# Attention with two expert layers on one core: routing's intermediate values move into spare PSUM columns of the banks of the product with v

## The chip, the cores and the metric

The kernel runs on one core of a Trainium2 chip. The metric is the device time of one execution in microseconds (us). The core's engines run side by side, each through its own list of instructions in order: TensorE (PE, matrix products into PSUM), VectorE (DVE), ScalarE (ACT), GpSimd (POOL) and SyncE (SP, which issues most DMAs). They wait for each other by semaphores only.

## The reference, cut to what matters

```python
def reference(q, k, v, moe_w_gate, moe_w_output_gate, moe_w1, moe_w2, moe2_w_in, moe2_w_out):
    attn_out = causal_attention(q, k, v)          # 4 batches, 12 heads, 448 tokens, head size 64
    x = tokens by (head, size)                    # 1792 x 768
    logits = x @ w_gate                           # 8 experts
    e_idx = argmax(logits, axis=1)
    gate_w = softmax(logits)[e_idx]
    eom = 1 / (1 + exp(-(x @ w_output_gate)))
    for e in range(8):
        m = e_idx == e
        out[m] = gate_w[m] * eom[m, e] * (relu(x[m] @ w1[e]) @ w2[e])
    h = out @ w_in
    return (h - tanh(h)) @ w_out
```

## The kernel before, in words

The work has three stages. The first is attention (up to some 232 us of the profiled span), the second the eight experts over the tokens that were sent to each, the third the last layer, whose products are the end of the program.

Attention goes through 24 units (`u`, two heads of one batch each, six units to a batch). The unit loop is a pipeline written out by hand: in each round `u` there are six steps `m`, and in every step the engines are given a piece of several units: the scores of unit `u` (`s_mm`, L328 and L329), the transposes of the exponentials of unit `u - 1` (`t_mm`, L361), the product with v of unit `u - 2` (`v_mm`, L380), and the transposes and logits of units `u - 3` and `u - 4` (`g_mm` L429, `g_lg` L440 and L441). DVE takes row maxima (L335), copies odd transposes (L367) and divides (L391, L394, L398); ACT takes the exponentials (L343), copies even transposes (L369, L431) and scales the second head (L402); POOL splits values into high and low halves (L302, L408, L409) and prepares weights (L117, L131). The order of the instructions on each engine is the order of this code; nothing reorders it.

The product with v of a unit has two result tiles, one for each head `h`, `[112, 4, 65]` in float32, 260 of the 512 columns of a PSUM bank. Steps 0 to 2 write head 0 (`VM` and `VO` set this), steps 3 to 5 head 1. Both come from the pool `ps_o` with two buffers, so head 0 always gets one bank and head 1 the other.

After a batch's last logits are added up (L447, L449), `routing(b)` runs for that batch as a generator: each `yield` ends a piece, and the loop takes one piece at every even step, in rounds `u` = 9 to 13 for the first batch, 15 to 19 for the second and 21 onwards for the third; the fourth (`b` = 3) runs after the last unit without other attention work beside it. The pieces are: add high and low logits, take the maximum (L453, L455); exponentials and comparison (L459 to L463); the one-hot choice (L466, L468); the running rank by matmuls and three DVE operations (L490 to L499); rank to place (L503 to L506); the weight of the token (L473 to L482, with an exponential on ACT at L476); the index table (L512 to L536). The intermediate values `lg`, `eq`, `es`, `rk`, `pi` and `pf` are tiles of the SBUF pool `sm`, three buffers each, as are `mx`, `ex`, `m2`, `eo`, `sx` and `bi`.

Of the kernel before, what the change touches and what calls it, by code (L numbers as in the profile page):

```python
# [12 lines left out]
F32 = mybir.dt.float32  # L13
F16 = mybir.dt.float16
BF16 = mybir.dt.bfloat16
I32 = mybir.dt.int32
# [4 lines left out]
PSUM = bass.MemoryType.PSUM  # L21
SP = mybir.EngineType.SP

B, H, S, D = 4, 12, 448, 64
CP, NCH = 112, 4
NT, DM = B * S, H * D
E, F1 = 8, 1024
# [32 lines left out]
def build(ctx: ExitStack, tc: tile.TileContext, kq0, kq, v, wg, wo, w1, w2, wf, out):  # L60
# [120 lines left out]
    with ExitStack() as actx:  # L181
# [3 lines left out]
        sm = sctx.enter_context(tc.tile_pool(reuse_waits="tile", name="sm", bufs=3, side="right"))  # L185
# [50 lines left out]
        NS = HU * S  # L236
        ps_s = actx.enter_context(tc.tile_pool(reuse_waits="tile", name="ps_s", bufs=3, space=PSUM))
        ps_t = actx.enter_context(tc.tile_pool(reuse_waits="tile", name="ps_t", bufs=3, space=PSUM))
        ps_o = actx.enter_context(tc.tile_pool(reuse_waits="tile", name="ps_o", bufs=2, space=PSUM))

        def views(z):
            stage = (raw1.rearrange("p a b -> p (a b)")[:, 2048:] if z % 2 else raw2.rearrange("p a b -> p (a b)"))
# [128 lines left out]
        def v_mm(u, h, i):  # L371
            d = st_[u]
            hl = (u % 2) * 2 + h
            if ("o", h) not in d:
                d["o", h] = ps_o.tile([128, 512], F32, tag="o", name=f"o_{u}_{h}")[:CP, 0 : NCH * (D + 1)].rearrange(
                    "p (c d) -> p c d", c=NCH)
            po = d["o", h]
            for j in range(i + 1):
                g, o = where[(h, i, j)]
                nc.tensor.matmul(out=po[:, i, :], lhsT=d["PT"][:, g, o : o + CP], rhs=d["t"][3][:, hl, j, :], start=(j == 0),  # L380
                                 stop=(j == i))
# [67 lines left out]
                nc.vector.tensor_tensor(out=lga, in0=lga, in1=plg, op=ALU.add)  # L449

        def routing(b):
            lg = sm.tile([CP, NCH, 2 * E], F32, tag="lg", name=f"lg_{b}")
            nc.vector.tensor_tensor(out=lg, in0=lga[:, :, 2 * E :], in1=lga[:, :, 0 : 2 * E], op=ALU.add)  # L453
            mx = sm.tile([CP, NCH, 1], F32, tag="mx", name=f"mx_{b}")
            nc.vector.tensor_reduce(out=mx, in_=lg[:, :, 0:E], op=ALU.max, axis=AX.X)  # L455
# [2 lines left out]
            ex = sm.tile([CP, NCH, E], F32, tag="ex", name=f"ex_{b}")  # L458
            nc.vector.tensor_tensor(out=ex, in0=lg[:, :, 0:E], in1=mxb, op=ALU.subtract)  # L459
            nc.scalar.activation(out=ex, in_=ex, func=AF.Exp, scale=1.0 / LSC)  # L460
            eq = sm.tile([CP, NCH, E], F32, tag="eq", name=f"eq_{b}")
            nc.vector.tensor_tensor(out=eq, in0=lg[:, :, 0:E], in1=mxb, op=ALU.is_equal)
            nc.vector.tensor_tensor(out=eq, in0=eq, in1=desc.unsqueeze(1).to_broadcast([CP, NCH, E]), op=ALU.mult)  # L463
            yield
# [6 lines left out]
            def weight():  # L471
                eo = sm.tile([CP, NCH, E], F32, tag="eo", name=f"eo_{b}")
                nc.vector.tensor_tensor(out=eo, in0=lg[:, :, E:], in1=ohb, op=ALU.mult)  # L473
                es = sm.tile([CP, NCH, 1], F32, tag="es", name=f"es_{b}")
                nc.vector.tensor_reduce(out=es, in_=eo, op=ALU.add, axis=AX.X)
                nc.scalar.activation(out=es, in_=es, func=AF.Exp, scale=-1.0 / LSC)  # L476
                sx = sm.tile([CP, NCH, 1], F32, tag="sx", name=f"sx_{b}")
                nc.vector.tensor_reduce(out=sx, in_=ex, op=ALU.add, axis=AX.X)
                yield
                nc.vector.tensor_scalar(out=es, in0=es, scalar1=1.0, scalar2=YSC, op0=ALU.add, op1=ALU.mult)  # L480
                nc.vector.scalar_tensor_tensor(out=es, in0=sx, scalar=1e-9, in1=es, op0=ALU.add, op1=ALU.mult)
                nc.vector.reciprocal(out=tm[:, b * NCH : (b + 1) * NCH, 1:2], in_=es)  # L482
                yield
# [7 lines left out]
            for c in range(NCH):  # L491
                nc.tensor.matmul(out=prv[:, c + 1 :, :], lhsT=onesb[:CP, :CP],
                                 rhs=oh[:, b, c : c + 1, :].to_broadcast([CP, NCH - c, E]), start=False, stop=(c == NCH - 1))
            rk = sm.tile([CP, NCH, E], F32, tag="rk", name=f"rkm_{b}")
            nc.vector.tensor_tensor(out=rk, in0=prv[:, 0:NCH, :], in1=base.unsqueeze(1).to_broadcast([CP, NCH, E]), op=ALU.add)
            nc.vector.tensor_tensor(out=rk, in0=rk, in1=oh[:, b, 0:NCH, :], op=ALU.mult)
            rb = rank[:, b * NCH : (b + 1) * NCH]
            nc.vector.tensor_reduce(out=rb.unsqueeze(2), in_=rk, op=ALU.add, axis=AX.X)
            nc.vector.tensor_tensor(out=base, in0=base, in1=prv[:, NCH, :], op=ALU.add)  # L499
            yield  # L500
            pi = sm.tile([CP, 3, NCH], I32, tag="pi", name=f"pi_{b}")
            pf = sm.tile([CP, 2, NCH], F32, tag="pf", name=f"pf_{b}")
            nc.vector.tensor_copy(out=pi[:, 0, :], in_=rb)  # L503
            nc.vector.tensor_scalar(out=pi[:, 2, :], in0=pi[:, 0, :], scalar1=7, scalar2=None, op0=ALU.logical_shift_right)
            nc.vector.tensor_scalar(out=pi[:, 1, :], in0=pi[:, 0, :], scalar1=127, scalar2=None, op0=ALU.bitwise_and)
# [2 lines left out]
            if b < B - 1:  # L508
                yield from weight()
# [4 lines left out]
            e = nc.vector if b >= B - 2 else nc.gpsimd  # L514
# [92 lines left out]
        for u in range(NU + 5):  # L607
# [20 lines left out]
            for m in range(6):  # L628
# [21 lines left out]
                if ok(u - 2):  # L650
                    for z in VM[m]:
                        v_mm(u - 2, *VO[z])
# [47 lines left out]
                if ok(u - 4) and (u - 4) % 6 == 5 and m == 2:  # L700
                    route = routing((u - 4) // 6)
# [561 lines left out]
    for q in range(2):  # L1263
        to_f32([(qc[q][:, h], stg[q][:, h, :]) for h in HS])
        for z in range(2):
            for h in HS:
                c = qc[q][:, h].bitcast(F32)
# [110 lines left out]
    for n in range(NF + 3):  # L1378
        g, f = divmod(n, KF2)
# [87 lines left out]
```

## Time and profile before

| | us |
|---|---|
| median of 3 runs | 1032.12 |
| lowest and highest | 1030.98, 1037.31 |
| the profiled execution, its own time | 1036.02 |
| its span, first to last instruction | 1034.3 |

| engine | busy us | share of the span | instructions |
|---|---|---|---|
| PE (matmul) | 981.5 | 95% | 8985 |
| PEld (weight loads of PE) | 735.5 | 71% | 8985 |
| DVE | 785.0 | 76% | 1704 |
| ACT | 604.1 | 58% | 1213 |
| POOL | 467.3 | 45% | 504 |

A row of the timeline gives the start, the time that the instruction or group took, the engine, the line, the operation, the result and its inputs, and in brackets how long the engine had sat idle before it and what ended that. Matmuls overlap each other, so their times add to more than they take together. An idle time is put down to the last of the things waited for.

### The profile page before, as it was taken

Reading aid. Unit: us, or ns where it says so; the run is one execution under the profiler, and the core shown is the slowest. Engines: PE = TensorE matmul, PEld = TensorE weight load, DVE = VectorE, ACT = ScalarE, POOL = GpSimd, SP = SyncE. Lnnn points to the kernel's source line nnn. Section 1 sums busy time; section 2 is a strip of 40 time slices with the busy share of each in tenths; the row PEclk is TensorE's granted clock in tenths of the full one; section 3 lists DMA queues with packets and bytes.
Section 4 is the critical chain, followed back from the end, with each engine's and each line's share of the span. In section 5 each row is a group of like instructions: output and inputs, shape, how many; then the busy total and the mean of one; then the engine's idle time right before and its main releaser. Section 6 shows DMA issues by size and latency. Waiting matters only on the chain. (4 is left out here: it accounts for less than half of the span.)

```text
span 1034.3 us, 23797 instructions
## 1 busy us (share of the span) xinstructions
PE 981.5 (95%) x8985; PEld 735.5 (71%) x8985; DVE 785.0 (76%) x1704; ACT 604.1 (58%) x1213; POOL 467.3 (45%) x504
## 2 busy tenths in 40 slices
PE   5989999999899998998998899999999999999996
PEld 3989999988678786686876455666666666667763
DVE  6647878787887778668886999887888798776640
ACT  5658887765456365564334698565556566555530
POOL 5466776575211021122136689645544443443321
PEclk9979999999999999999999999999999999999999
DMA  8888999954998988988986360010000000000000
GB/s 244 232 200 232 268 263 224 258 188 144 327 338 333 359 277 303 339 295 300 323 321 220 130 273 1 31 40 16 23 32 31 8 32 8 16 16 16 16 24 23
DMA packets 62648, 173.94 MB, mean 168 GB/s; under 512 B 8368, under 2 KB 23344, under 8 KB 59424
## 3 DMA queue, kind: packets, MB, share of 16 engines
q1 hardware_dynamic: 56352, 147.20, 42.5%
q0 software_dynamic: 6144, 24.84, 8.7%
q8 instruction: 80, 1.31, 0.5%
q14 instruction: 72, 0.59, 0.2%
HBM read 132.30 MB, written 29.62 MB: 157 GB/s over the span
## 5 line engine op out<-in xcount | busy, mean ns | idle before, releaser
L1361 PE MATMUL fo<-wo,g 128*128 128x384 f16 x1344 | 228.2, 326 | 0.0
L1310 PEld LDWEIGHTS <-raw 128*128 128x128 f16 x1440 | 141.2, 98 | 86.7 <-issue 9.0
L1361 PEld LDWEIGHTS <-g 128*128 128x128 f16 x1344 | 131.2, 98 | 83.8
L1320 POOL TENSOR_TENSOR V<-cu,cc 128x384 f32<-128x384 f32 (+1 forms) x80 | 80.1, 1001 | 188.0 <-ACT cu L1319 185.4
L164 PEld LDWEIGHTS <-w 128*128 128x128 f16 x2592 | 146.0, 98 | 9.5 <-issue 8.1
L1310 PE MATMUL fh<-cu,raw 128*128 128x384 f16 (+1 forms) x864 | 133.1, 310 | 4.6 <-DVE cc L1318 3.4
L380 PE MATMUL o<-v,PT 112*112 112x65 f32 x960 | 119.4, 266 | 0.0
L343 ACT ACTIVATE P<-s,nb 112x112 f32<-112x112 f32 (+1 forms) x192 | 89.8, 495 | 49.5 <-DVE nb L335 24.9
L380 PEld LDWEIGHTS o<-v,PT 112*112 112x112 f32 x960 | 110.3, 185 | 0.2
L123 DVE SCALAR_TENSOR_TENSOR w<-raw,w 128x768 f16<-128x768 f32 (+1 forms) x99 | 99.0, 1060 | 11.4 <-ACT w L115 11.4
L335 DVE CUSTOM_DVE_ANT_0 s<-s,maskw 112x112 f32<-112x112 f32 (+1 forms) x192 | 85.8, 459 | 21.4 <-PE s L329 18.4
L811 POOL DMA_INDIRECT xg<-xs_d,idx x22 | 30.7, 1397 | 155.9 <-PEq L886 36.5
L1319 ACT ACTIVATE cu<-cc 128x384 f32<-128x384 f32 (+1 forms) x80 | 40.0, 500 | 93.9 <-DVE cc L1318 93.9
L115 ACT ACTIVATE w<-raw 128x768 f16<-128x768 f32 (+2 forms) x106 | 89.4, 904 | 6.7 <-DMA raw<-w 3.9
L1318 DVE TENSOR_TENSOR cc<-fh,co 128x384 f32<-128x384 f32 (+1 forms) x80 | 42.0, 525 | 63.5 <-PE fh L1310 50.8
L1323 POOL TENSOR_TENSOR X<-cc,X 128x384 f32<-128x384 f32 (+1 forms) x80 | 87.6, 1094 | 4.1 <-ACT X L1322 0.5
L1330 DVE SCALAR_TENSOR_TENSOR V<-cu,V 128x384 f32<-128x384 f32 (+1 forms) x80 | 82.6, 1032 | 0.1
L1338 DVE TENSOR_TENSOR V<-V,co 128x384 f32<-128x384 f32 (+1 forms) x64 | 77.5, 1211 | 0.0
L361 PE MATMUL t<-ident,P 112*112 112x112 f32 x480 | 69.3, 268 | 0.0
L1310 PE MATMUL fh<-yh,raw 128*128 128x384 f16 x384 | 67.6, 326 | 0.7 <-DVE cc L1318 0.7
L1339 ACT ACTIVATE g<-V 128x384 f16<-128x384 f32 (+1 forms) x80 | 40.0, 500 | 45.9 <-DVE V L1338 45.7
L328 PE MATMUL s<-kh,qa 128*112 128x112 f16 (+1 forms) x192 | 54.4, 302 | 12.8 <-POOL qa L280 7.3
(670 smaller groups left out, 1978.3 us busy)
## 6 DMA issues: line engine op xcount, KB each, us to landing
raw<-w SPq DMA_DIRECT2D x48, 512.0 KB
raw<-w SPq DMA_DIRECT2D x60, 384.0 KB
cu<-wf SPq DMA_DIRECT2D x22, 1024.0 KB
wb_d<-co SPq DMA_DIRECT2D x22, 512.0 KB
raw<-kq SPq DMA_DIRECT2D x11, 896.0 KB
raw<-wb_d SPq DMA_DIRECT2D x8, 768.0 KB
xs_d<-xq SPq DMA_DIRECT2D x24, 224.0 KB
raw<-v SPq DMA_DIRECT2D x11, 448.0 KB
```

What stands on the lines that cost most here:

```text
L115: nc.scalar.activation(out=out, in_=in_, func=AF.Copy, scale=WS)
L123: nc.vector.scalar_tensor_tensor(out=out, in0=in_, scalar=WS, in1=hi, op0=ALU.mult, op1=ALU.subtract)
L164: nc.tensor.matmul(out=ph[:, (f % 4) * 128 : (f % 4 + 1) * 128], lhsT=w[0][:, ww, k, f * 128 : (f + 1) * 128], rhs=xTs[tag][:, xx, k, :], ...
L335: nc.vector.tensor_tensor_reduce(out=d["s", m][:, z, :], in0=d["s", m][:, z, :], in1=maskw[:, S - n : S], scale=-0.125, scalar=3.0e38, op0 ...
L343: nc.scalar.activation(out=d["P"][:, j, OFF[i] : OFF[i] + n], in_=d["s", m][:, z, :], func=AF.Exp, bias=d["nb"][:, 2 * i + j : 2 * i + j + ...
L380: nc.tensor.matmul(out=po[:, i, :], lhsT=d["PT"][:, g, o : o + CP], rhs=d["t"][3][:, hl, j, :], start=(j == 0), stop=(j == i))
L1310: nc.tensor.matmul(out=ph[:, 0:nt], lhsT=wi[ww][:, f // 4, k, f % 4 * 128 : (f % 4 + 1) * 128], rhs=yy[:, k, 0:nt], start=(q == 0), stop=( ...
L1320: nc.gpsimd.tensor_tensor(out=d["V"], in0=d["U"], in1=d["h"], op=ALU.mult)
L1323: nc.gpsimd.tensor_tensor(out=d["X"], in0=d["h"], in1=d["X"], op=ALU.subtract)
L1330: nc.vector.scalar_tensor_tensor(out=d["V"], in0=d[f"S{z}"], scalar=QD[z - 1], in1=d["V"], op0=ALU.add, op1=ALU.mult)
L1338: nc.vector.tensor_tensor(out=d["V"], in0=d["V"], in1=rs_y(g, nt), op=ALU.mult)
L1361: nc.tensor.matmul(out=po[:, 0:384], lhsT=t[:, x, k, i * 128 : (i + 1) * 128], rhs=wo_[ww][:, k, z * 384 : (z + 1) * 384], start=(k == 0 a ...
```

## The change

Routing's `lg`, `eq`, `es`, `rk`, `pi` and `pf` are no longer SBUF tiles. They lie in columns 320 to 475 of the PSUM bank that holds head 0 of the product with v. The two result tiles of that product, until now a new pair from a rotating pool for every unit, become two tiles that are made once, `o_0` and `o_1`. Each value has one place now where it had three buffers.

```diff
-        ps_o = actx.enter_context(tc.tile_pool(reuse_waits="tile", name="ps_o", bufs=2, space=PSUM))
+        ps_o = actx.enter_context(tc.tile_pool(reuse_waits="tile", name="ps_o", bufs=1, space=PSUM))
+        o_ps = [ps_o.tile([128, 512], F32, name=f"o_{h}") for h in range(2)]
+        small = lambda o, n: o_ps[0][:CP, 320 + o : 320 + o + n]
...
-                d["o", h] = ps_o.tile([128, 512], F32, tag="o", name=f"o_{u}_{h}")[:CP, 0 : NCH * (D + 1)].rearrange(
-                    "p (c d) -> p c d", c=NCH)
+                d["o", h] = o_ps[h][:CP, 0 : NCH * (D + 1)].rearrange("p (c d) -> p c d", c=NCH)
...
-            lg = sm.tile([CP, NCH, 2 * E], F32, tag="lg", name=f"lg_{b}")
+            lg = small(0, NCH * 2 * E).rearrange("p (c e) -> p c e", c=NCH)
...
-            eq = sm.tile([CP, NCH, E], F32, tag="eq", name=f"eq_{b}")
+            eq = small(64, NCH * E).rearrange("p (c e) -> p c e", c=NCH)
...
-                es = sm.tile([CP, NCH, 1], F32, tag="es", name=f"es_{b}")
+                es = small(128, NCH).unsqueeze(2)
...
-            rk = sm.tile([CP, NCH, E], F32, tag="rk", name=f"rkm_{b}")
+            rk = small(96, NCH * E).rearrange("p (c e) -> p c e", c=NCH)
...
-            pi = sm.tile([CP, 3, NCH], I32, tag="pi", name=f"pi_{b}")
-            pf = sm.tile([CP, 2, NCH], F32, tag="pf", name=f"pf_{b}")
+            pi = small(132, 3 * NCH).bitcast(I32).rearrange("p (a n) -> p a n", a=3)
+            pf = small(144, 2 * NCH).rearrange("p (a n) -> p a n", a=2)
```

No engine's instructions change their order. What changes is which of them wait, since routing's values now share a bank with the products with v. In the rows below the names with a number are tiles; `o_172` is `o_0`, the fixed tile of head 0. The lines of the changed kernel are one or two higher than those of the kernel before.

On PE, in round 11 of the unit loop, the end of step 1, first before and then after; `lg_1691` and `lg_1668` are the logits of a later unit, `v_4` and `PT` the inputs of the product with v of unit 9:

```order
L440 LDWEIGHTS xh_1634
L440 MATMUL lg_1691<-wgc,xh_1634 128x32
L441 LDWEIGHTS xh_1634
L441 MATMUL lg_1691<-wgc,xh_1634 112x16
L380 MATMUL o_0_1662<-v_4_957,PT_1475 112x65 x3
L328 LDWEIGHTS qa_1001
L328 MATMUL s_2_1709<-kh_1002,qa_1001 112x336 [waits Activation_49]
```

```order
L441 LDWEIGHTS xh_1613
L441 MATMUL lg_1668<-wgc,xh_1613 128x32
L442 LDWEIGHTS xh_1613
L442 MATMUL lg_1668<-wgc,xh_1613 112x16
L381 MATMUL o_172<-v_4_950,PT_1459 112x65 [waits Activation_49]
L381 MATMUL o_172<-v_4_950,PT_1459 112x65 x2
L330 LDWEIGHTS qa_993
L330 MATMUL s_2_1686<-kh_994,qa_993 112x336
```

The product with v, which waited for nothing here, waits for ACT (for the exponential of `es`, L476), and the next scores, which waited for ACT, need no wait of their own any more.

On DVE, in the same round, the end of step 0 with the first operations of the token's weight, first before and then after; `rs_1` belongs to the division of head 1, `o_173` is `o_1`, `eo`, `oh`, `sx` and `ex` are still SBUF tiles:

```order
L391 TENSOR_SCALAR rs_1_1668<-o_1_1583 112x4
L394 RECIPROCAL rs_1_1668<-rs_1_1668 112x4 [waits DVE_49]
L473 TENSOR_TENSOR eo_1671<-lg_1403,oh 112x32
L475 TENSOR_REDUCE es_1673<-eo_1671 112x4 [waits DVE_49]
L478 TENSOR_REDUCE sx_1676<-ex_1446 112x4
```

```order
L392 TENSOR_SCALAR rs_1_1646<-o_173 112x4
L395 RECIPROCAL rs_1_1646<-rs_1_1646 112x4 [waits DVE_49]
L474 TENSOR_TENSOR eo_1649<-o_172,oh 112x32 [waits PE_49]
L476 TENSOR_REDUCE o_172<-eo_1649 112x4 [waits DVE_49]
L479 TENSOR_REDUCE sx_1653<-ex_1431 112x4
```

`eo`, which waited for nothing, waits for PE (for the product with v of step 0), because its input `lg` now lies in the bank that this product writes.

## Rows read from the trace of the kernel before

**Rows 1.** The page, part 1: busy us of each engine (share of the span) xinstructions.

```profile
PE 981.5 (95%) x8985; PEld 735.5 (71%) x8985; DVE 785.0 (76%) x1704; ACT 604.1 (58%) x1213; POOL 467.3 (45%) x504
```

**Rows 2.** Windows: length, then busy us (instructions) of PE, PEld, DVE, ACT, POOL; clock, DMA.

```profile
133.00:180.00 47.00, 45.71 (x504) 43.11 (x503) 38.51 (x153) 35.99 (x90) 32.70 (x38) 1.00 0.95 251
```

**Rows 3.** Waits between 90 and 260 us: waiter <- waited for: us, times, longest.

```profile
PEld t L361 <- ACT PT L369: 0.6, 2, 0.3
...
PE s L328 <- ACT P L343: 0.6, 2, 0.3
...
PE rk L490 <- DVE oh L468: 0.5, 1, 0.5
...
PE xt L429 <- DVE base L499: 0.2, 1, 0.2
```

**Rows 4.** DVE groups by shape, 90 to 260 us: busy us, mean ns | idle before.

```profile
L496 DVE TENSOR_TENSOR rkm<-rkm,oh 112x32 f32<-112x32 f32 x4 | 5.0, 1253 | 0.1
...
L453 DVE TENSOR_TENSOR lg<-lga 112x64 f32<-112x64 f32 x4 | 3.6, 894 | 0.1
...
L462 DVE TENSOR_TENSOR eq<-lg,mx 112x32 f32<-112x32 f32 x4 | 2.2, 546 | 0.0
...
L463 DVE TENSOR_TENSOR eq<-eq,desc 112x32 f32<-112x32 f32 x4 | 1.7, 422 | 0.1
L473 DVE TENSOR_TENSOR eo<-lg,oh 112x32 f32<-112x32 f32 x4 | 1.7, 415 | 0.0
...
L504 DVE TENSOR_SCALAR pi<-pi 112x4 int32<-112x4 int32 x4 | 1.3, 334 | 0.1
...
L506 DVE CAST pf<-pi 112x8 f32<-112x8 int32 x4 | 1.2, 303 | 0.1
...
L495 DVE TENSOR_TENSOR rkm<-rk,base 112x32 f32<-112x32 f32 x4 | 0.8, 192 | 1.4 <-PE rk L492 1.3
...
L475 DVE TENSOR_REDUCE es<-eo 112x4 f32<-112x32 f32 x4 | 0.7, 186 | 0.1
```

**Rows 5.** Timeline, second batch's rank: DVE, then POOL, then PE.

```profile
157.46 2.51 DVE L496 TENSOR_TENSOR rkm<-rkm,oh 112x32 f32<-112x32 f32 x1
...
158.04 1.88 POOL L302 TENSOR_TENSOR lo<-raw,t 128x896 f16<-128x896 f32 x1
...
160.41 0.55 PE L429 MATMUL xt<-identh,xq 112*128 112x112 f16 x8 [0.25 <-DVE base L499]
```

**Rows 6.** Timeline, second batch's weight: PE, then ACT.

```profile
164.12 0.78 PE L380 MATMUL o<-v,PT 112*112 112x65 f32 x6
165.21 0.30 PE L328 MATMUL s<-kh,qa 128*112 128x336 f16 x1 [0.31 <-ACT P L343]
...
165.66 0.20 ACT L476 ACTIVATE es<-es 112x4 f32<-112x4 f32 x1
```

**Rows 7.** Timeline, first batch: choice (DVE, PE), then weight (DVE, ACT, PE).

```profile
102.98 0.19 DVE L468 TENSOR_TENSOR oh<-eq,m 112x32 bf16<-112x32 f32 x1
...
103.21 0.78 PE L380 MATMUL o<-v,PT 112*112 112x65 f32 x6
...
111.00 0.82 DVE L473 TENSOR_TENSOR eo<-lg,oh 112x32 f32<-112x32 f32 x1
...
112.08 0.21 ACT L476 ACTIVATE es<-es 112x4 f32<-112x4 f32 x1 [0.89 <-DVE es L475]
...
111.78 0.78 PE L380 MATMUL o<-v,PT 112*112 112x65 f32 x6
```

**Rows 8.** Timeline of PE: first scores of rounds 17, 18, 21 and 22.

```profile
161.90 0.21 PE L328 MATMUL s<-kh,qa 128*112 128x112 f16 x1
...
170.94 0.21 PE L328 MATMUL s<-kh,qa 128*112 128x112 f16 x1
...
196.03 0.21 PE L328 MATMUL s<-kh,qa 128*112 128x112 f16 x1
...
204.32 0.21 PE L328 MATMUL s<-kh,qa 128*112 128x112 f16 x1
```

## The prediction

> **What bounds the kernel now.** I read the page's busy times first. PE is busy for 95% of the span, the next engine, DVE, for 76% [rows 1]. The change touches attention alone, so I then read the windows of that stage: between 133 and 180 us, a stretch that holds nearly all of the routing of the second batch, PE is busy for 45.71 of 47 us at full granted clock, DVE for 38.51 [rows 2]. The reader is to see that PE sets the pace there and that DVE, which does nearly all of routing, has some 8 us to spare in 47. What DVE saves is therefore worth only what PE waits for because of DVE, and the list of waits is the third view. Between 90 and 260 us PE lost little to DVE or ACT: twice 0.3 us for exponentials of L343, twice 0.3 us for a copy of L369, 0.2 us for the running base of L499, and 0.5 us for the one-hot choice of the last batch [rows 3].
>
> The fourth view, the groups by shape, tells why DVE is late at all. L496 multiplies 32 columns and takes 1253 ns on average, L495, the same operation on the same shape just before it, 192 ns [rows 4]. They differ in one thing: L495 has one input in PSUM and one in SBUF, L496 both in SBUF. The timeline shows the disturbance: the L496 of the second batch runs from 157.46 for 2.51 us and ends 0.05 us after POOL's L302, which works on SBUF from 158.04 for 1.88 us [rows 5]. L462, L463, L473, L504 and L506 are long in the same way [rows 4].
>
> **What the change removes.** In L462, L463, L473 and L496 one of two SBUF inputs becomes a PSUM input, in L504 and L506 everything lies in PSUM. If they then behave like L495, the four cost 192 ns each. Over four batches that is (1253 - 192) x 4 = 4.2 us for L496, (546 - 192) x 4 = 1.4 for L462, 0.9 for L463 and 0.9 for L473. For L504 and L506, against the 186 ns of the small reduction L475, it is (334 - 186) x 4 = 0.6 and 0.5. The sum is 8.5 us of DVE time [rows 4]. L453 keeps both inputs in SBUF and stays at 894 ns.
>
> Of these 8.5 us PE gets only what it waited for. Round 17 of the unit loop, in which the second batch's weight is computed, takes 170.94 - 161.90 = 9.04 us, round 21, without such a wait, 204.32 - 196.03 = 8.29 us [rows 8]. The 0.75 us between them hold one each of the 0.3 us waits for L343 and L369, whose other halves fall in the third batch [rows 3]. So I count 0.75 us twice, and 0.2 us for L499, which came late because of the long L496 [rows 3, 5]: 1.7 us gained, at most.
>
> What would a write to PSUM cost? No row shows a small DVE operation with input and output in PSUM. The nearest rows are L495 (PSUM to SBUF, 192 ns) and L475 (SBUF to SBUF, 186 ns) [rows 4]: no difference that matters, and I take none. From below, nothing can make them much shorter than that; from above I allow 50 ns on each of some 20 operations, 1 us of DVE time per batch, which the 8 us that DVE has to spare in rows 2 hide in the first three batches. In the last one six of them stand ahead of the choice that PE waits for [rows 3], 0.3 us.
>
> [...]
>
> **What the change adds.** No instruction moves; waits are added, since the values share a bank with head 0 of the product with v. Three kinds matter.
>
> First, DVE waits for PE: L453, L466, L473 and L480 wait for the last product into that bank. Behind them stand DVE's copies and row maxima, for which ACT waits. In the first batch L473 began at 111.00 after the product with v of step 0, so this costs nothing when DVE is on time.
>
> Second, PE waits for DVE: the products of head 0 at steps 0 and 1 wait for L463, L468, L506 and L517 where they waited for the division L398 or for nothing. Behind them stands all of PE. The closest is the choice: L468 ended at 102.98 + 0.19 = 103.17 and the product began at 103.21 [rows 7]. The margin is 0.04 us. I take 0.1 us a batch for it, 0.3 us in all; from below it is 0, with the time saved at L462 and L463 ahead of it.
>
> Third, PE waits for ACT: the product of step 1 in the weight's round waits for the exponential L476, which waits for L475 and L473. In the first batch L476 began at 112.08 and the product at 111.78, so as things stand this is a new wait of 112.29 - 111.78 = 0.5 us. But L473 took 0.82 us there, and ACT had sat idle for 0.89 us until L475 came [rows 7]. With L473 at 0.19 us the chain is 111.00 + 0.19 + 0.19 + 0.21 = 111.59, before the product. I take 0.1 us a batch, 0.3 us in all.
>
> The waits of DVE for itself, and the 1.4 KB per partition that become free (three buffers of 480 bytes) and shift other tiles, I cost at nothing: nothing else is placed or loaded differently, and DVE's spare time covers the first. The fourth batch has no product with v beside it and takes none of the three waits.
>
> **The sum.** -1.7 + 0.3 + 0.3 = -1.1 us on the profiled execution's 1036.02 us, that is 1034.9. The profiled execution lies 3.9 us above the median of the runs shown, 1032.12; the same step from the median gives 1031.0. The runs themselves spread over 6.3 us (1030.98 to 1037.31), so about 1%, 10 us, is what a measurement of this kernel can tell from no change, and this is far less.
>
> **Rivals.**
>
> The new waits win (slower). Place: the product with v of step 1 in the weight's round, behind L476. Point: it decides as soon as L475 ends more than 0.19 us later than in the chain above (111.78 - 111.59), because DVE stays late, be it by L453, which keeps its length, or because an operation with one SBUF operand is still held up by POOL. This second reason means that the change does not do what it says. Price, with DVE as late as before: in the second batch the product can start only at 165.66 + 0.20 = 165.86 instead of 164.12, and the scores behind it after its 0.78 us at 166.64 instead of 165.21, 1.4 us [rows 6]; the third batch as much, the first 0.5 us: 3.3 us. The products of step 0 and the choice can add as much again, 6.6 us. Midway, +5 us: 1041 by the profile, 1037 on the median's scale. For it speaks that in rows 6 ACT is late on its own account too; against it, that rows 7 show the chain in time but for one disturbed operation.
>
> [...] That the program guards the whole bank is seen in the order of PE, where the product got a wait for columns it does not touch; no trace here shows what would happen without.
>
> All of PE's idle time goes (faster). DVE early by 8.5 us might also shorten waits that are put down to POOL or ACT. The cap is PE's idle time in the window, 47 - 45.71 = 1.3 us for a batch [rows 2], 3.9 us for three; taking 3 us gives 1029. Against it: part of that idle time is issue and the wait for POOL's halves, which the change leaves alone.
>
> The time saved in attention is lost again behind it, since the experts' weights come at their own pace: 0 us, 1032.1. Nothing in rows 2 speaks against it; it cannot be told from the forecast.
>
> **How the numbers follow.** Chances: forecast 0.5 (its own range 1029 to 1034), saved and lost again 0.2, new waits win 0.18, all idle time goes 0.12. All of them lie within 1% of 1032.12 by their price. For a median of few runs I add 2 us on either side of 1029 and 1 us above 1037: 1027 to 1038. More than 10 us faster would need more than the 8.5 us of DVE time that is to be had, chance 0.03, left for what I have not seen; more than 10 us slower would need the dearest form of the waits and half as much again, 0.04; within 1%: 0.93.
>
> **What would show it right or wrong.** In the changed kernel's profile L496 (one line lower) should take about 192 ns in all four batches, like L462, L463 and L473, while L453 stays long; busy DVE should fall by some 8 us and busy PE stay. Round 17 should take about 8.4 us. PE's list of waits should have new rows of a few tenths for L380 on ACT L476 and DVE L468. If DVE's operations are still over a microsecond, the first part is wrong; if L380 waits over 1 us a batch, the second; if the time differs by over 10 us, something outside attention changed, and the whole reading is wrong.

## The result and the profile after

| | kernel before | changed kernel |
|---|---|---|
| median of 6 runs each, us | 1034.79 | 1021.13 |
| lowest and highest, us | 1030.98, 1037.31 | 1016.89, 1022.43 |
| ratio to before, 95% interval | | 0.9866, 0.9838 to 0.9894 |
| the profiled execution, its own time and its span, us | 1036.02, 1034.3 | 1016.89, 1015.2 |

The changed kernel is faster by 1.3%. The forecast was 1031.0 us, the range 1027 to 1038: both are wrong. The operations did what was forecast of them. What their lateness had cost was read much too low.

The page of the changed kernel, part 1, answers to [rows 1]:

```profile
PE 971.3 (96%) x8985; PEld 728.7 (72%) x8985; DVE 776.7 (77%) x1704; ACT 604.1 (60%) x1213; POOL 462.4 (46%) x504
```

DVE is busy for 8.3 us less, the forecast's 8. PE, which was to stay, is busy for 10.2 us less with the same 8985 matmuls. The same matmuls in less busy time point to the clock, and this is the first sign of what the prediction left out: over the whole span the mean granted clock is 0.982 before and 0.991 after. Most of that difference lies in one place of this profile of before, round 6, to which the first experiment comes.

DVE's groups by shape between 90 and 260 us, as in [rows 4] (lines are one or two higher, a result named `o` lies in the fixed tile):

```profile
L454 DVE TENSOR_TENSOR o<-lga 112x64 f32<-112x64 f32 x3 | 2.5, 847 | 0.4 <-PE o L381 0.4
L496 DVE TENSOR_TENSOR o<-rk,base 112x32 f32<-112x32 f32 x4 | 0.8, 200 | 1.7 <-PE rk L493 1.7
L464 DVE TENSOR_TENSOR o<-o,desc 112x32 f32<-112x32 f32 x4 | 0.8, 199 | 0.1
L497 DVE TENSOR_TENSOR o<-o,oh 112x32 f32<-112x32 f32 x4 | 0.8, 199 | 0.1
L463 DVE TENSOR_TENSOR o<-o,mx 112x32 f32<-112x32 f32 x4 | 0.8, 197 | 0.0
L507 DVE CAST o<-o 112x8 f32<-112x8 int32 x4 | 0.7, 174 | 0.1
L505 DVE TENSOR_SCALAR o<-o 112x4 int32<-112x4 int32 x4 | 0.7, 170 | 0.1
L474 DVE TENSOR_TENSOR eo<-o,oh 112x32 f32<-112x32 f32 x4 | 0.7, 163 | 0.0
```

Each of these but L454 takes 163 to 200 ns, where they took up to 1253. L454, the old L453, has both inputs in SBUF still and is still long.

The timeline of the second batch's rank, DVE and POOL, answers to [rows 5]: L497 takes 0.20 us beside the same operation of POOL that held it for 2.51 us before.

```profile
147.91 0.20 DVE L497 TENSOR_TENSOR o<-o,oh 112x32 f32<-112x32 f32 x1
...
148.01 1.89 POOL L304 TENSOR_TENSOR lo<-raw,t 128x896 f16<-128x896 f32 x1
```

PE's list of waits between 90 and 260 us, as in [rows 3] (waiter, waited for, us, times, longest):

```profile
PE pt_I-4341_4342 L151 <- DMA xg<-xs_d,idx: 1.5, 1, 1.5
PE py_I-4366_4367 L176 <- issue: 0.6, 1, 0.6
PE rk L491 <- DVE oh L469: 0.5, 1, 0.5
PE s L331 <- DMA kl<-lo: 0.3, 1, 0.3
PE px L531 <- DVE bb L522: 0.2, 1, 0.2
```

The waits for ACT's exponentials, for its copies and for the running base are gone; the one of the last batch's choice stays at 0.5 us. The product with v (L381) is not in the list, whose shortest row is 0.2 us: none of the waits that the change added holds PE for longer than that. A wait that [rows 3] do not show is gone too. In the same list of before it was the longest one of PE for DVE:

```profile
PE px L530 <- DVE bb L521: 0.8, 1, 0.8
```

It stands before the product that starts the third batch's index table. The 0.2 us of L531 that the list after shows belong to the fourth batch.

The window of 47 us with the second batch, as in [rows 2] (PE busy, then PEld, DVE, ACT, POOL, clock, DMA):

```profile
125.00:172.00 47.00, 46.62 (x526) 44.77 (x524) 36.20 (x156) 37.13 (x94) 32.25 (x36) 1.00 0.96 249
```

PE's idle time falls from 1.29 to 0.38 us. That is 0.9 us for a batch, the size that the prediction had in mind. So between these two profiles the routing of the second batch explains very little of the 13 us, and the experiments had to find the rest.

### The profile page after: what moved, and what is told of

Its sections match the earlier page's. It is cut to its first block, busy times and chain, and to the rows that moved or that the text cites. A ratio compares the mean times of both kernels' runs of the same rounds, so it can differ in the third digit from the quotient of the medians.

```text
span 1015.2 us, 23805 instructions
## 1 busy us (share of the span) xinstructions
PE 971.3 (96%) x8985; PEld 728.7 (72%) x8985; DVE 776.7 (77%) x1704; ACT 604.1 (60%) x1213; POOL 462.4 (46%) x504
## 5 line engine op out<-in xcount | busy, mean ns | idle before, releaser
L381 PE MATMUL o<-v,PT 112*112 112x65 f32 x960 | 115.3, 260 | 0.0
L381 PEld LDWEIGHTS o<-v,PT 112*112 112x112 f32 x960 | 106.1, 179 | 0.3
L812 POOL DMA_INDIRECT xg<-xs_d,idx x22 | 27.0, 1228 | 153.1 <-PEq L887 29.5
```

## The experiments

All of them are read by one yardstick as well: the time from the first scores of round 10 to those of round 19, in which the routing of the first two batches runs. The length of a round is the difference between the starts of its first scores and of the next round's, as in [rows 8].

| kernel | routing's values in | rounds 10 to 18, us | clock there | round 11 | round 17 | DVE busy, page |
|---|---|---|---|---|---|---|
| before | SBUF | 78.37 | 1.00 | 8.82 | 9.04 | 785.0 |
| again | SBUF | 85.45 | 0.94 | 11.51 | 13.19 | 788.3 |
| again2 | SBUF | 86.39 | 0.94 | 14.95 | 11.36 | 792.0 |
| fixed_only | SBUF | 80.91 | 1.00 | 9.80 | 9.92 | 788.2 |
| shift_only | SBUF | 80.18 | 0.98 | 8.29 | 11.57 | 785.2 |
| fill | SBUF | 80.77 | 1.00 | 10.05 | 9.99 | 789.5 |
| rk_only | one of six in PSUM | 78.83 | 1.00 | 8.64 | 9.84 | 786.1 |
| all_but_rk | five of six in PSUM | 78.19 | 1.00 | 8.68 | 8.51 | 777.5 |
| late | PSUM | 79.86 | 1.00 | 9.58 | 9.86 | 781.8 |
| changed | PSUM | 76.81 | 1.00 | 8.42 | 8.52 | 776.7 |
| changed_again | PSUM | 76.71 | 1.00 | 8.42 | 8.51 | 777.0 |
| changed_pad | PSUM | 75.93 | 1.00 | 8.44 | 8.51 | 776.7 |
| lg_copy | PSUM | 79.17 | 1.00 | 8.29 | 8.94 | 777.1 |
| lg_copy2 | PSUM | 78.49 | 1.00 | 8.29 | 8.51 | 776.4 |

### The kernel before, profiled again (again, again2)

The span of before held one dear event that has nothing to do with routing. In round 6, in which no routing runs, PE waited for a DMA, and its clock then fell (timeline of PE, and in the second fence two windows of before with the clock in the third column from the right):

```profile
61.73 0.25 PE L329 MATMUL s<-kl,qa 128*112 128x112 f16 x1 [2.59 <-DMA kl<-lo]
```

```profile
60.00:70.00 10.00, 8.27 (x51) 8.09 (x52) 3.03 (x14) 3.62 (x11) 3.74 (x6) 0.56 0.93 239
70.00:80.00 10.00, 10.00 (x88) 9.36 (x87) 5.52 (x22) 5.17 (x13) 5.92 (x7) 0.76 0.86 219
```

Round 6 took 17.2 us instead of 8.3. The first question was whether the change removes this, whether its fixed tiles or addresses matter, or whether it is an accident of that execution. The first repetition asked this, together with the three kernels of the next section:

> The kernel before, unchanged, to see whether the wait of 2.6 us for the transfer of kl at round 6 and the half clock behind it (1.2 GHz until about 75 us, round 6 17.2 us instead of 8.3) belong to it. Theory A (the gain of the changed kernel is this one wait and its clock, taken away by a steady part of the change): round 6 takes about 17 us here too, time ratio 1.00. Theory B (the wait is an accident of one profiled execution): round 6 takes 8.3 us here, and the ratio is still 1.00, so that the 13 us of the changed kernel must come from elsewhere.

Measured: 1031.58 us (10 runs, 1025.16 to 1038.49), ratio 1.0019 (0.9975 to 1.0063). Round 6 took 8.30 us here, and in every other profile between 8.30 and 8.53. The event was an accident of one execution, and not what the change removes.

But two other rounds were dear, 11 and 17, both with the weight of a token. The second repetition had a theory of this on record, theory D: operations of routing with their inputs in SBUF make DVE late, and PE waits behind it. Theory B has the first measurement of the changed kernel as an accident.

> The kernel before, unaltered, another profile. Theory D: PE waits for ACT or DVE by 0.3 to 1.5 us in at least one of rounds 11, 14, 16 and 17, and rounds 10 to 18 take 78 to 86 us together. Theory B: rounds 10 to 18 take 75.5 to 77.5 us, like the changed kernel.

Measured: 1032.17 us (12 runs), ratio 1.0003 (0.9965 to 1.004), rounds 10 to 18 in 86.39 us, 0.4 us above the range that the theory of late operations expected. Its timeline shows the mechanism at its clearest, in round 11: DVE, then POOL, then ACT, then PE.

```profile
100.25 0.17 DVE L504 TENSOR_SCALAR pi<-pi 112x4 int32<-112x4 int32 x1
100.33 1.88 DVE L505 TENSOR_SCALAR pi<-pi 112x4 int32<-112x4 int32 x1
102.24 3.07 DVE L506 CAST pf<-pi 112x8 f32<-112x8 int32 x1
105.22 0.62 DVE L335 CUSTOM_DVE_ANT_0 s<-s,maskw 112x448 f32<-112x448 f32 x1
...
100.29 1.89 POOL L302 TENSOR_TENSOR lo<-raw,t 128x896 f16<-128x896 f32 x1 [2.59 <-DMA xs_d<-xq]
...
103.33 1.89 POOL L302 TENSOR_TENSOR lo<-raw,t 128x896 f16<-128x896 f32 x1
...
105.93 0.63 ACT L343 ACTIVATE P<-s,nb 112x448 f32<-112x448 f32 x1 [4.59 <-DVE nb L335]
...
106.61 0.30 PE L328 MATMUL s<-kh,qa 128*112 128x336 f16 x1 [3.01 <-ACT P L343]
```

L505 and L506 work on 4 and 8 columns. L505 ends at 102.21, 0.03 us after the first L302 of POOL, L506 at 105.31, 0.09 us after the second. The row maxima (L335) behind them come late, ACT sits idle for 4.59 us and PE for 3.01. The two are no exceptions: in the six profiles with all of routing's values in SBUF, 120 of routing's operations on at most 64 columns take more than 0.35 us between 80 and 262 us, and every one of them ends between 0.02 us before and 0.16 us after the end of an instruction of POOL. No run took POOL's work away, so that POOL is what holds them rests on these ends, and on the operations that became short when their values moved. Then the clock falls (windows of again2):

```profile
106.00:108.00 2.00, 1.39 (x12) 1.08 (x11) 1.90 (x12) 1.94 (x7) 0.00 (x0) 0.98 1.13 283
108.00:114.00 6.00, 6.00 (x30) 5.28 (x30) 4.66 (x19) 4.79 (x12) 5.01 (x6) 0.50 1.01 347
114.00:116.00 2.00, 2.00 (x23) 1.87 (x22) 0.69 (x2) 0.98 (x2) 1.89 (x3) 0.81 1.07 338
```

For 6 us and a part of the next two PE is never idle, and yet its granted clock is 0.50, the lower of the two values that the clock takes in the traces of before and of the changed kernel (0.50 and 1.00). What this means for PE is seen in the trace of before: products of 448 columns (L328, L329) that follow each other without a pause start 0.37 us apart at a clock of 0.50 (from 71.80 us) and 0.19 us apart at 1.00 (from 149.75 us), that is 1.2 and 2.4 columns per ns. The 1.2 GHz of the expectations stands for the first of these rates. In the changed kernel the same place reads (timeline of DVE):

```profile
100.47 0.17 DVE L506 TENSOR_SCALAR o<-o 112x4 int32<-112x4 int32 x1
100.67 0.17 DVE L507 CAST o<-o 112x8 f32<-112x8 int32 x1
100.79 0.63 DVE L337 CUSTOM_DVE_ANT_0 s<-s,maskw 112x448 f32<-112x448 f32 x1
```

The row maximum begins at 100.79 instead of 105.22, with the first scores of the round at 100.67 in both.

The windows of rounds 11 and 17 in again, and then in again2, let the price be added up:

```profile
100.13:111.64 11.51, 10.47 (x95) 9.38 (x95) 11.01 (x35) 8.01 (x20) 9.79 (x10) 0.85 0.92 236
155.21:168.40 13.19, 11.93 (x95) 10.70 (x94) 10.69 (x38) 7.11 (x18) 5.87 (x7) 0.74 1.03 255
```

```profile
100.67:115.62 14.95, 11.94 (x95) 10.71 (x95) 12.54 (x36) 8.07 (x20) 11.65 (x13) 0.77 0.94 266
158.32:169.68 11.36, 10.07 (x94) 9.31 (x94) 10.23 (x37) 6.89 (x18) 5.01 (x7) 0.85 0.98 232
```

A round without a wait takes some 8.5 us. For the second row, 13.19 - 11.93 = 1.26 us of idle PE, and 0.26 of 13.19 us, 3.4 us, of missing clock: 8.5 + 1.3 + 3.4 = 13.2. For the third, 3.0 idle and 0.23 x 14.95 = 3.4 of clock: 14.9. What the clock took behind a wait was more than the wait itself: 3.4 us against 1.26 in the second row, 3.4 against 3.0 in the third.

### The fixed tiles alone, the addresses alone (fixed_only, shift_only, changed_pad)

fixed_only makes the two result tiles once, and leaves routing's values in SBUF:

```diff
-        ps_o = actx.enter_context(tc.tile_pool(reuse_waits="tile", name="ps_o", bufs=2, space=PSUM))
+        ps_o = actx.enter_context(tc.tile_pool(reuse_waits="tile", name="ps_o", bufs=1, space=PSUM))
+        o_ps = [ps_o.tile([128, 512], F32, name=f"o_{h}") for h in range(2)]
...
+                d["o", h] = o_ps[h][:CP, 0 : NCH * (D + 1)].rearrange("p (c d) -> p c d", c=NCH)
```

> Only the two fixed result tiles of the product with v; routing's values stay in SBUF, all addresses as before. Takes away one wait of PE for itself at round 3 and two late ones. Theory A1 (the fixed tiles shift the start): about 10 us faster, round 6 8.3 us. Theory A2 (the addresses of the attention tiles do it) and theory C (routing's operations do it): no change, within 2 us.

Measured: 1029.28 us (10 runs), ratio 0.9969 (0.9933 to 1.0005). Not told from 1.

shift_only keeps everything of before, but takes five of the six values from a pool on the other side of SBUF, so that what lay above them moves to the addresses that it has in the changed kernel:

```diff
+        vp = actx.enter_context(tc.tile_pool(reuse_waits="tile", name="vp", bufs=3, side="right"))
...
-            lg = sm.tile([CP, NCH, 2 * E], F32, tag="lg", name=f"lg_{b}")
+            lg = vp.tile([CP, NCH, 2 * E], F32, tag="lg", name=f"lg_{b}")
...
```

> The kernel before with lg, eq, es, pi and pf in an SBUF pool of their own below the others, so that all other attention tiles lie where they lie in the changed kernel; routing works as before. Theory A2 (the addresses do it): about 10 us faster, round 6 8.3 us. Theory A1 and theory C: no change, within 2 us.

Measured: 1029.62 us (10 runs), ratio 0.9973 (0.9942 to 1.0005). Not told from 1 either.

changed_pad is the changed kernel with an unused tile that shifts the addresses back to those of before:

```diff
+        sm.tile([CP, 128], F32, tag="pad", name="pad")
```

> The changed kernel with 1536 unused bytes per partition, so that the other attention tiles lie where they lay before. Theory A2: only routing's own 2 to 4 us are left of the gain (about 1031), round 6 17 us. Theory A1 and theory C: as fast as the changed kernel, about 1021, ratio 0.987.

Measured: 1021.0 us (6 runs), ratio 0.9911 (0.988 to 0.9943). The median is that of the changed kernel; by the ratio, to the kernel before on this run's own chip, 9 of some 14 us stay. The fixed tiles and the addresses do not make the gain: on the same chip fixed_only is 7.9 us slower than changed_pad in the mean of the runs (95% interval about 4 to 12 us). It is where routing's values lie. That the tiles or the addresses have a part of some us in it is not excluded by their intervals, which begin at 0.993 and 0.994.

### Which of the values (rk_only, all_but_rk)

rk_only has the fixed tiles and only `rk` in PSUM, all_but_rk is the changed kernel with `rk` back in SBUF:

```diff
-            rk = small(96, NCH * E).rearrange("p (c e) -> p c e", c=NCH)
+            rk = sm.tile([CP, NCH, E], F32, tag="rk", name=f"rkm_{b}")
```

> Fixed result tiles and rk alone in the spare columns; lg, eq, es, pi and pf in SBUF as before. Theory D (DVE late through routing's operations on two SBUF inputs makes PE wait, and behind a long wait PE runs at 1.2 GHz for some us): L496 at 0.19 us takes away half of the lost DVE time, the second batch is in time (rounds 16 and 17 near 8.55), the first still depends on L473; about 1025, ratio 0.993. Theory R (the new place and the new waits of the change do it, whatever DVE's lateness is): the wait for L476 and the other places are missing, so under half of the gain, 1029.

> The changed kernel with rk back in SBUF. Theory D: the multiply of L496 takes 1 to 2.5 us again where POOL reads SBUF beside it; rounds 10, 16 and 17 are longer by 0.3 to 3 us, sometimes with half clock; about 1026, ratio 0.995. Theory R: nearly the whole gain stays, about 1022, ratio 0.990.

Measured: rk_only 1026.52 us, ratio 0.9978 (0.9939 to 1.0016); all_but_rk 1024.51 us, ratio 0.997 (0.993 to 1.001), 10 runs each. The groups by shape show that each shortens the operations on the values that it moved, first rk_only, then all_but_rk:

```profile
L504 DVE CAST pi<-rank 112x4 int32<-112x4 f32 x4 | 4.3, 1087 | 0.0
...
L464 DVE TENSOR_TENSOR eq<-eq,desc 112x32 f32<-112x32 f32 x4 | 2.6, 655 | 0.1
...
L497 DVE TENSOR_TENSOR o<-o,oh 112x32 f32<-112x32 f32 x4 | 0.8, 199 | 0.1
```

```profile
L497 DVE TENSOR_TENSOR rkm<-rkm,oh 112x32 f32<-112x32 f32 x4 | 2.2, 538 | 0.1
L464 DVE TENSOR_TENSOR o<-o,desc 112x32 f32<-112x32 f32 x4 | 0.8, 199 | 0.1
```

In rounds 10 to 18 both lie between the changed kernel and the average of the six profiles with all values in SBUF (82.0 us), though not clearly below the first of them (78.37). By their ratios neither half alone can be told from before, while both halves together can. The changed kernel did not run on this chip, but lg_copy, which has all six values in PSUM (below), did: 1020.57 us, 6.0 us under rk_only and 3.9 under all_but_rk.

Neither theory came out whole. For rk_only the theory of late operations expected rounds 16 and 17 near 8.55 us, and they took 8.70 and 9.84; for all_but_rk it expected rounds 10, 16 and 17 to grow, and they took 8.66, 8.71 and 8.51, as in the changed kernel to within 0.2 us. The lines show why the half is no half. In the six profiles L496 takes 2.9 to 5.0 us in all, and with rk in PSUM it is short; yet busy DVE is 786.1 us, against 785.0 to 792.0 in the six. The cast behind it (L504, one input in SBUF) takes 1087 ns on average, where the six have 303 to 926. This fits a hold that passes to the next operation with its values in SBUF; single profiles spread too widely to show it. With all but rk moved busy DVE is 777.5 us.

### DVE made late in the changed kernel (late)

late gives DVE an unused reduction of 2.28 us in each of the first three batches, just behind the multiplication that was long before:

```diff
+            if b < B - 1:
+                late = sm.tile([CP, 16, 1], F32, tag="late", name=f"late_{b}")
+                nc.vector.tensor_reduce(out=late, in_=io128.unsqueeze(1).to_broadcast([CP, 16, 128]), op=ALU.max, axis=AX.X)
```

> The changed kernel with one more DVE reduction of some 2.3 us (one SBUF input, result unused) behind the multiply of rk in the first three batches, about as long as L496 took at its worst before; everything else as changed. Theory D: DVE is late again, PE waits 1 to 2 us at the new waits or for ACT in rounds 11, 17 and 23, with half clock behind some of these waits: 8 to 12 us slower than the changed kernel, 1029 to 1033, ratio about 1.00. Theory R: DVE's time does not matter, at most the waits themselves, 1 to 2 us: 1022, ratio 0.990.

Measured: 1025.81 us (10 runs, 1020.93 to 1033.64), ratio 0.9976 (0.9933 to 1.0019), 4.7 us above the median of the changed kernel and 5.2 above that of lg_copy on the same chip (in the means 5.5 us, 95% interval about 2 to 9). Its DVE group, and in the second fence PE's waits between 90 and 173 us:

```profile
L500 DVE TENSOR_REDUCE late<-io 112x16 f32<-112x2048 f32 x3 | 6.8, 2276 | 0.0
```

```profile
PE o L381 <- DVE o L510: 1.3, 2, 0.6
PE o L381 <- ACT o L477: 0.7, 2, 0.5
PE s L331 <- DMA kl<-lo: 0.3, 1, 0.3
```

6.8 us of late DVE, in a kernel in which DVE is busy for 76%, cost some 5 by the medians. The theory of late operations expected 8 to 12 and half clock behind some of the waits; the clock over rounds 10 to 18 stayed at 1.00. This run shows that lateness of DVE reaches PE also where POOL is not what makes it. But here it does so by the waits that the change added: these are the product with v on ACT's L477 and on DVE's L510, which is the rival "the new waits win". In the kernel before, the way was another, by ACT's exponentials, and that way is seen in the traces alone. In all_but_rk, where POOL can still hold the multiplication of rk, the same two waits take 0.4 and 0.2 us between 90 and 260 us. The added waits exist, and they cost little only because the change also makes DVE early.

### The last long operation (lg_copy, lg_copy2)

lg_copy copies the high logits into the spare columns, so that the sum L454, the only routing operation that stayed long, also has an input in PSUM:

```diff
-            nc.vector.tensor_tensor(out=lg, in0=lga[:, :, 2 * E :], in1=lga[:, :, 0 : 2 * E], op=ALU.add)
+            nc.vector.tensor_copy(out=lg, in_=lga[:, :, 2 * E :])
+            nc.vector.tensor_tensor(out=lg, in0=lg, in1=lga[:, :, 0 : 2 * E], op=ALU.add)
```

> The changed kernel with the last long operation shortened: the high half of the logits is first copied into the spare columns, so that the sum of L453 has one input in PSUM and one in SBUF; one more short DVE operation a batch. Theory D: the sum and the copy take 0.4 us together where the sum alone took 0.5 to 1.5 us; there is little lateness left to take away, 0 to 1 us faster than the changed kernel, about 1020.5. Theory R: no difference, or 0.3 us slower.

> The kernel that was run as lg_copy (the changed one, with the high logits copied into spare PSUM columns, so that the sum of high and low logits has one PSUM input) once more, on the same chip as the changed kernel. If what is left of DVE's lateness at that sum (775 ns against some 200, four times) still costs PE time: 1 to 3 us below the changed kernel, ratio 0.983 to 0.990 to the kernel before. If it is covered: the same as the changed kernel within 1.5 us.

Measured: 1020.57 us, ratio 0.9919 (0.9881 to 0.9957), and on the same chip as a repetition of the changed kernel 1021.95 us, ratio 0.9896 (0.9859 to 0.9933), against that one's 1019.72. The groups of lg_copy:

```profile
L455 DVE TENSOR_TENSOR o<-o,lga 112x64 f32<-112x64 f32 x3 | 0.7, 233 | 0.1
L454 DVE COPY o<-lga 112x64 f32<-112x64 f32 x3 | 0.7, 227 | 0.4 <-PE o L381 0.4
```

847 ns became 227 + 233, and nothing was gained: what is left of the lateness is covered. No version here beat the changed kernel.

In the table both profiles of lg_copy are 2 to 3 us longer over rounds 10 to 18 than the changed kernel. By the list DVE is not what PE waits for there. PE's waits of lg_copy between 90 and 172 us begin with a transfer:

```profile
PE s L331 <- DMA kl<-lo: 1.6, 3, 0.9
```

lg_copy2 has 1.7 us of it, the three profiles of the changed kernel 0.0 to 0.4, before 0.6, fixed_only 1.2. What makes this transfer late was not tested. So the yardstick holds more than DVE's lateness, and differences of a microsecond or two between single profiles are not to be read as the work of routing.

### PE kept busy, and the changed kernel again (fill, changed_again)

fill is fixed_only with 16 unused products in rounds 11, 17 and 23, where PE waits:

```diff
+                if (u, m) in ((11, 1), (17, 1), (23, 1)):
+                    for _ in range(16):
+                        nc.tensor.matmul(out=o_ps[0][:, 320:448], lhsT=identh, rhs=identh, start=True, stop=True)
```

> Only the two fixed tiles, routing's values in SBUF as before, and PE is given 16 unused products of 128 x 128 (about 1 us, an estimate from the 0.13 us that a product of this size takes of PE at most) at the end of step 1 of rounds 11, 17 and 23, just where it waits for the exponentials. If the granted clock behind the wait is the larger part of the gain: no stretch at 1.2 GHz in rounds 11 and 17, which take 8.5 to 9.6 us each, and a ratio of 0.991 to 0.996. If only the wait itself counts: a ratio of 0.997 to 1.001, as with the fixed tiles alone, since the products fill the wait and do not shorten it.

Measured: 1028.99 us (12 runs), ratio 0.9973 (0.9944 to 1.0001). Round 17 in fixed_only, then in fill:

```profile
153.59:163.51 9.92, 8.66 (x95) 7.96 (x94) 9.60 (x36) 6.54 (x18) 4.58 (x6) 1.00 0.96 225
```

```profile
153.96:163.95 9.99, 9.55 (x110) 8.87 (x110) 9.67 (x36) 6.52 (x18) 4.65 (x6) 1.00 1.01 248
```

The products fill the wait (idle PE 0.44 instead of 1.26 us) and the round is as long as before. The theory by which the clock is the larger part expected 0.991 to 0.996 and missed; the direct wait counts for more than I had come to think. The run doesn't say how much the clock counts, since fixed_only's own profile had no fall of the clock there that the products could have kept away.

> The changed kernel unaltered, a second set of times and a second profile. Theory D (operations with two SBUF inputs make DVE late, PE waits for ACT behind it in the rounds of the token's weight, and a stretch at 1.2 GHz can follow): ratio 0.985 to 0.993 to the kernel before; rounds 11 and 17 take 8.3 to 8.6 us, with no stretch at 1.2 GHz in rounds 10 to 18, and rounds 10 to 18 together 75.5 to 77.5 us. Theory B (the first measurement was an accident): ratio 0.995 to 1.002, and rounds 11 or 17 over 9 us.

Measured: 1019.72 us (6 runs, 1017.06 to 1023.62), ratio 0.9866 (0.983 to 0.9901), rounds 11 and 17 in 8.42 and 8.51 us, no fall of the clock in rounds 10 to 18. The theory's numbers came out; the first measurement was no accident.

### Where the time went

By the three measured ratios (0.9866 twice, 0.9911 with the pad) the changed kernel is some 9 to 14 us faster, and three parts of that were found.

First, late DVE in rounds 10 to 18, without any fall of the clock: before, fixed_only and fill took 78.37, 80.91 and 80.77 us, on average 80.0, the three profiles of the changed kernel 76.5. That is 3.5 us, of which some 0.6 are the longer waits for the transfer of kl (0.6, 1.2 and 0.6 us against 0.0 to 0.4).

Second, the routing of the third batch, from the first scores of round 23 to the product that starts its index table (L530, L531 after). The windows of before, then of after:

```profile
212.88:225.20 12.32, 11.27 (x123) 10.29 (x122) 11.93 (x46) 9.10 (x22) 10.46 (x14) 1.00 0.47 132
```

```profile
202.09:212.65 10.56, 10.56 (x123) 10.18 (x123) 9.65 (x39) 8.25 (x22) 9.88 (x14) 1.00 0.49 147
```

DVE was busy for 11.93 of 12.32 us: in this stretch it was DVE that set the pace, and PE's wait of 0.8 us for L521 at its end, steady at 0.7 to 0.8 us in all six profiles, is a part of it. 1.76 us go, and now PE is busy throughout. The other profiles with the values in SBUF have 12.1 to 12.4 us here, those of the changed kernel 10.5 to 10.6.

Third, the clock. Every run lists its mean granted clock. The 72 runs of before that the later comparisons use have a mean time of 1030.7 us and a mean clock of 0.9866; 18 runs of the changed kernel (with changed_pad) have 1020.3 us and 0.9901. Taking only runs with a clock of 0.989 to 0.991, it is 1028.1 us (17 runs) and 1020.5 (8 runs). So of 10.3 us about 7.6 remain at equal clock, and 2.7 go with the clock. This is a comparison of groups, not a run that changed the clock alone.

3.5 + 1.76 is 5.3 us of the 7.6. The 2.3 us between them were not located in this way.

The averages of the six profiles with all values in SBUF and of the three of the changed kernel, with the falls of the clock left in, say where the time went more directly. The spans differ by 10.3 us. Rounds 10 to 18 take 82.0 against 76.5 us, the third batch's stretch 12.3 against 10.6: 7.3 us lie in these two. Rounds 19 to 22 differ by 0.3 us, and the work behind the last batch's index table by 0.8 (783.8 against 783.0, where single profiles range from 780 to 789). The last 2.0 us lie ahead of round 10, and 1.5 of them are the accident of round 6, shared among six profiles. How much of the 5.5 us of rounds 10 to 18 is the clock's depends on how often it falls: it did so in again, again2 and shift_only, and in none of the five profiles with all six values in PSUM and nothing added to delay DVE.

## Why the prediction was wrong

**Right: the operations.** Of the four it said "192 ns each": they took 163 to 199, L505 and L507 170 and 174 for 186, and L453 stayed long. The write to PSUM, which the prediction took at no cost, cost little: the two whose result alone went there, L476 and L496, took 195 and 200 ns, where before L475 took 186 and L495 192. Round 17 took 8.52 us, forecast "about 8.4".

**Right, with one bit too much: the added waits.** 0.6 us were set aside for them, and no row of L381 is in PE's list of the changed kernel. The waits of DVE for PE that were foreseen do show, 1.2 us in all at L454 and L481, and PE pays nothing for them that its list shows. The argument by [rows 7], that the chain is in time once L473 is short, held. late shows that its condition was the right one.

**Wrong: "Of these 8.5 us PE gets only what it waited for ... 1.7 us gained, at most."** That is the step that failed: the term of 1.7 us stands where the medians show 13.7 us and the ratios 9 to 14. It failed in three ways.

It took one execution for all. What POOL does when an operation of routing begins differs from run to run, and with it which operation is held and for how long: L506 has a mean of 303 ns in [rows 4] and took 3.07 us in again2. The waits of [rows 3], twice 0.3 us for the exponentials, were 2.5 us in again and 4.6 in again2 over the same window:

```profile
PE s L328 <- ACT P L343: 2.5, 3, 1.3
```

```profile
PE s L328 <- ACT P L343: 4.6, 3, 3.0
```

I happened to read the mildest of the profiles: 78.37 us against 80 to 86. The 8 us of DVE time to be saved were therefore too low as well; against again2 the page shows 792.0 - 776.7 = 15.3. The three times on record, which spread over 6.3 us, were a hint that one profile is one draw.

It had no price for the clock. The profile that I read held the price in full: in round 6 a wait of 2.59 us, then clocks of 0.56 and 0.76 and 9 us lost. I looked at windows of the stretch of routing alone, whose clock was 1.00 [rows 2], and so counted a microsecond of waiting as a microsecond.

It took the second batch for all batches. "PE sets the pace there" and DVE "has some 8 us to spare in 47" is true of 133 to 180 us. In the third batch's stretch, at 213 to 225 us, DVE was busy for 97%, and some 1.7 us were lying there in each of the six profiles with the values in SBUF. A window by batch would have shown it, and so would the list of waits: the row of L530, 0.8 us, is in the window of [rows 3] and larger than any wait that the prediction counted, and it was left out of the sum without a reason.

The last sign, "if the time differs by over 10 us, something outside attention changed", follows from the same step and is wrong with it: the time differs by over 10 us, and the stretches that grew shorter lie in attention.

**The rivals.** "All of PE's idle time goes" had the right direction, with a cap of 1.3 us a batch that suffers from the same faults. That the time is "saved and lost again" is wrong: the stages behind gave nothing back that the profiles or the medians show. "The new waits win" is wrong here, and its mechanism is real, as late shows.

**The chances.** "More than 10 us faster would need more than the 8.5 us of DVE time that is to be had" carried the chance of 0.03, and it fails with the first two faults: more DVE time was to be had (8 to 15 us against the several profiles), and a wait can cost PE more than its own length, as in round 17 of again: 1.26 us idle and 3.4 us of missing clock.

## What to carry to other kernels

Price a late engine by its worst draws and not by the mean of one profile: where an operation of 0.2 us takes 1 to 3 beside another engine's, look at which engine waits if it is hit at the worst place, and read the window of each batch, not of one. Where the profile shows that TensorE's clock fell behind a wait, count what the clock took along with the wait. Small values that DVE reads beside a busy POOL were worth keeping in PSUM here, by 9 to 14 us, where columns of a bank were spare and the added waits lay on engines that were early; and they were worth it together, since half of them gave less than could be told from nothing.

## What the runs showed of the hardware that was not expected

Operations of DVE on 4 and 8 columns in SBUF ran on until an operation of POOL on SBUF had ended, even with a single input: in again2 L505 took 1.88 us and L506 3.07, and they ended 0.03 and 0.09 us after one of POOL's L302; in the changed kernel, with input and output in PSUM, each took 0.17. The prediction had counted two such operations among the long ones, at 303 and 334 ns, and had explained the length by two SBUF inputs; a single operation ten times as long was not in its rows. By the ends of POOL's operations a cast (L506, 3.07 us), a tensor-scalar (L505, 1.88) and two-input operations (L496, 2.51 in the profile of before) were held. The reductions L475 and L498, which read and write SBUF, took 186 ns in each of the four batches of before; whether a reduction can be held was not tested.

The granted clock fell to 0.50 behind a wait of 1.26 us (round 17 of again, 0.74 over the round) and stayed at 1.00 behind one of the same length (round 17 of fixed_only, 1.26 us too). What decides between the two was not tested.
